# Decode attention with a gated FFN: splitting TensorE's value pass around the first tile's scores, and moving the last semaphore clear

## The chip, the cores and the metric

The kernel runs on one core of a Trainium2 chip. The metric is the device time of one execution in microseconds (us), as the median of several runs. A separate execution was taken with the hardware profiler; its times are used wherever a single instruction or a stretch of the run is spoken of. One core has TensorE (PE, matrix products into PSUM), VectorE (DVE), ScalarE (ACT), GpSimd (POOL) and SyncE (SP, which here only issues DMAs). All engines run on their own and meet at semaphores.

## The reference

One token `x` (512 values) goes through two branches that are mixed by a scalar gate.

```python
q = (x @ wq) as 32 heads of 128
scores = einsum("bhqd,bhkd->bhqk", q, k_cache) * 128 ** -0.5     # 32 heads x 65536 keys
p = softmax(scores); o = einsum("bhqk,bhkd->bhqd", p, v_cache)   # 65536 values of 128 per head
a = o.reshape(1, 1, 4096) @ wo
b = (silu(x @ w_gate) * (x @ w_up)) @ w_down
out = g * a + (1 - g) * b,   g = sigmoid(sum(x * gate_w))
```

Everything is bfloat16. The two caches are 537 MB each (32 x 65536 x 128 x 2 bytes), and every byte of them is read once.

## The kernel before: how the work is tiled and staged

A **tile** is 16384 keys of one head (128 partitions x 128 keys x 128 values of a key), and four tiles make a head. Two tiles make a **pair**, 8.39 MB, and a head is two pairs. There are 128 tiles and 64 pairs for K and as many for V. On chip there are two K buffers of a pair each (`K_bufs`) and one V buffer of a pair (`V_buf`, in two halves of 4.19 MB).

**Scores of a tile** (VectorE, then TensorE, then VectorE). `product` (L264) multiplies the tile by the head's query, in place. `add_halves` (L275) adds the upper half of the 128 products of each key to the lower one: 128 to 64, to 32, and the last time to 16 columns, which go into a small tile `T_sb`. `scores` (L446) lets TensorE add those 16 columns in groups of four, by four matmuls with a unit matrix, into `S_ps`, and `fold` (L286) adds the last four columns on VectorE and writes the scores to `S_sb`. `T_sb` is a single buffer: the last addition of a tile waits for the scores of the tile before (`wait(dve, pe_S, n)`).

**Softmax and values** run one head behind the scores. VectorE takes the head's maximum (L292), TensorE turns it (L460), ScalarE makes the exponentials of two tiles at a time (`P_sb`, L365), and TensorE multiplies them by V: `values` (L467) is 32 matmuls for each half of V, so 64 for a pair.

**TensorE runs a loop** (`tensor_step`) of 61 turns, one for each pair from the third to the last but one. Within a turn its order is fixed, and `take(credit)` makes the whole engine wait for another engine's credit: first `c_S[0]` (tile 0's `T_sb`), then `c_q`, `c_P` (the exponentials), `c_V` twice (a half of V has landed; GpSimd passes this on, `tell_of_v`), `c_S[1]` (tile 1's `T_sb`), `c_o` and `c_m`.

**SP issues all large DMAs in a fixed order** on one queue. In the turn for pair m, `sync_step` issues the V load of pair m - 1, then the K load of pair m + 2. K's load (L174) waits until both tiles' scores of pair m are made, since it takes the place of that pair. V's load differs by parity. For a pair with an **even** number one DMA of 8.39 MB (L174) waits until *both* halves of the V pair before have been used. For an **odd** one two DMAs of 4.19 MB (L178) go out as each half comes free. In this order the queue sees, over one head: V (whole pair), K, V (half), V (half), K.

```python
    def load_v(i):
        for n in (2 * i, 2 * i + 1):
            wait(sync, pe_V, n - 1 if i % 2 else 2 * i)
            if i % 2:
                load_tile(V_half[n % 2], A_v_cache, n, (vA_in, vB_in)[n % 2])
        if i % 2 == 0:
            load_pair(V_buf, A_v_cache, i, vA_in)
```

The turns thus come in two kinds, which the text calls by what TensorE reads in them. In the **pair turn** V comes in one DMA of 8.39 MB, and behind it the two half loads are issued; in the **halves turn** V comes in two DMAs, and behind it the whole pair is issued.

**Start and end.** The prologue makes q, the gate, the FFN and the first four tiles' scores. `tensor_end` does the last pair with its own finer loads, projects with `wo`, and SP stores 1 KB of output (L230). Then GpSimd waits for three engines and for the output's landing, and clears all semaphores (L692).

Of the kernel before, what the change touches and what calls it, by code (L numbers as in the profile page):

```python
# [11 lines left out]
NB = 128  # L12
# [29 lines left out]
def kernel(  # L42
# [14 lines left out]
    nc = tc.nc  # L57
# [21 lines left out]
    def sb(name, shape, dtype=f32):  # L79
        return consts.tile(shape, dtype, name=name)  # L80
# [11 lines left out]
    P_sb = sb("P_sb", [P, PAIR], bf16)  # L92
# [33 lines left out]
    def halves(buf):  # L126
        return [buf[:, i * NB * Dh : (i + 1) * NB * Dh].rearrange("p (j d) -> p j d", d=Dh) for i in range(2)]

    K_half, V_half = [halves(b) for b in K_bufs], halves(V_buf)
# [3 lines left out]
    def v_view(n):  # L133
        return {N - 4: K_half[0][1], N - 3: V_half[0], N - 2: V_half[1], N - 1: K_half[1][1]}[n]

    sync, act, dve, pool, pe = nc.sync, nc.scalar, nc.vector, nc.gpsimd, nc.tensor
    first_sem = nc.alloc_semaphore("first")
    done = Events(nc, "done")
    po, pe_x, pe_S, pe_V, pe_q, pe_m, pe_t, pe_o = (
        Events(nc, n) for n in ("po", "pe_x", "pe_S", "pe_V", "pe_q", "pe_m", "pe_t", "pe_o")  # L140
    )
    ac, ac_q, dv, dv_top, dv_max, dv_rg = (
        Events(nc, n) for n in ("ac", "ac_q", "dv", "dv_top", "dv_max", "dv_rg")
    )
    x_in, gw_in, wq_in, kb_in, wg_in, wu_in, wd_in, vA_in, vB_in, out_in = (
        Events(nc, n, 16)
        for n in ("x_in", "gw_in", "wq_in", "kb_in", "wg_in", "wu_in", "wd_in", "vA_in", "vB_in", "out_in")
    )
    k_in = [Events(nc, f"k{i}_in", 16) for i in range(2)]
    v4_in = Events(nc, "v4_in", 16)  # L150
# [5 lines left out]
    c_q, c_P, c_V, c_o, c_m = (nc.alloc_semaphore(n) for n in ("c_q", "c_P", "c_V", "c_o", "c_m"))  # L156
# [4 lines left out]
    def wait(engine, events, value):  # L161
        key = id(engine), id(events)
        if seen.get(key, 0) < value:
            engine.wait_ge(events.sem, value)
            seen[key] = value
# [40 lines left out]
    def sync_step(m):  # L206
        load_v(m - 1)
        if m + 2 < M:
            wait(sync, pe_S, 2 * m + 2)
            load_k(m + 2)  # L210
# [16 lines left out]
    def sync_out():  # L227
        wait(sync, dv, dv.n)
        wait(sync, ac, ac.n)
        out_in(sync.dma_start(out=out[0], in_=out_sb))  # L230


    def unit_matrix():
# [19 lines left out]
    def product(n):  # L253
        K = K_half[n // 2 % 2][n % 2]
        q = q_sb[n // G % 2]
        q_rep = bass.AP(tensor=q.tensor, offset=q[:, :].offset, ap=[list(q[:, :].ap[0]), [0, NB], [1, Dh]])
        m = n // 2

        if m in (0, M - 1) and n % 2:
            wait(dve, kb_in, 16 if m == 0 else 32)  # L260
        else:
            wait(dve, k_in[m % 2], 16 * (m // 2 + 1))
        wait(dve, ac_q, n // G + 1)
        return dv(dve.tensor_tensor(out=K, in0=K, in1=q_rep, op=ALU.mult))  # L264

    def add_halves(n, width, last, out=None):
        K = K_half[n // 2 % 2][n % 2]
        half, mark = Dh // 2, last
        while half >= width:
            wait(dve, dv, mark)  # L270
            to = K[:, :, 0:half]
            if half == width and out is not None:
                wait(dve, pe_S, n)
                to = out
            ins = dve.tensor_tensor(out=to, in0=K[:, :, 0:half], in1=K[:, :, half : 2 * half], op=ALU.add)  # L275
            if half == width and out is not None:
                ins.then_inc(c_S[n % 2], 1)
            else:
                mark = dv(ins)
            half //= 2  # L280
        marks["K", n] = mark

    def fold(n):
        h, g = divmod(n, G)
        wait(dve, pe_S, n + 1)
        return dv(dve.tensor_reduce(  # L286
            out=S_sb[h % 2][:, g * NB : (g + 1) * NB], in_=S_ps[n % 2], axis=AXIS.X, op=ALU.add
        ))

    def row_max(h, folded):  # L290
        wait(dve, dv, folded)
        dv_max(dve.tensor_reduce(out=m_sb[:, 0:1], in_=S_sb[h % 2], axis=AXIS.X, op=ALU.max))  # L292

    def top_of(h):
        wait(dve, pe_m, 2 * h + 1)
        dv_top(dve.tensor_reduce(out=top[:, 0:1], in_=mT, axis=AXIS.X, op=ALU.max))  # L296

    def weight(h, t):
        wait(dve, pe_t, t)
        if h < H - 1:  # L300
            wait(dve, dv, dv(dve.tensor_reduce(out=tsum[:, 0:1], in_=tot, axis=AXIS.X, op=ALU.add)))
            total = tsum[:, 0:1]
        else:
            total = tot[:, 0:1]
        wait(dve, dv, dv(dve.reciprocal(recip[:, 0:1], total)))
        dv_rg(dve.tensor_tensor(out=rg[:, h : h + 1], in0=recip[:, 0:1], in1=gval, op=ALU.mult))

    def vector_step(m):
        h, b = divmod(m, MH)
        width, to = (WIDTH, T_sb) if m < M - 1 else (LAST, None)  # L310
        last = product(2 * m)
        if b == 0:
            top_of(h - 1)
        else:
            fold(2 * m - 1)
        add_halves(2 * m, width, last, to)
        last = product(2 * m + 1)
        fold(2 * m)
        if b == 1:
            weight(h - 1, m - 1)  # L320
        add_halves(2 * m + 1, width, last, to)
        if b == 1:
            row_max(h, fold(2 * m + 1))

    def vector_end():
        top_of(H - 1)
        weight(H - 1, M - 1)
        wait(dve, pe_x, 5)
        dv(dve.tensor_copy(out=out_sb[:, :HD], in_=a_ps[0]))  # L329
# [71 lines left out]
    def scalar_step(m):  # L401
        h, b = divmod(m, MH)
        if b == 0:
            head_bias(h - 1)
        wait(act, pe_V, 2 * (m - 2))
        exponentials(h - 1, b, P_sb, PAIR).then_inc(c_P, 1)
        if m == M - 1:
            return
        if b == 1:
            query(h + 1, True)  # L410
        else:
            act.sem_inc(c_q, 1)
        wait(act, pe_V, 2 * (m - 2) + 2)
        o_copy(h - 1).then_inc(c_o, 1)
        wait(act, pe_o, m - 1)
        if b == 0:
            marks["half_o"] = ac(copy(half_o[:, 0:1], oh))
            act.sem_inc(c_m, 1)
        else:
            ac(head_out(h - 1, add_half_o()))  # L420
            head_diag(h, True)
# [18 lines left out]
    def take(credit):  # L440
        pe.wait_ge(credit, 1)
        pe.sem_inc(credit, -1)  # L442

    def scores(n, src, width):
        for c in range(0, width, QUAD):
            ins = pe.matmul(  # L446
                S_ps[n % 2], lhsT=ident_b, rhs=src[:, :, c : c + QUAD],
                start=(c == 0), stop=(c == width - QUAD),
            )
        pe_S(ins)  # L450
# [5 lines left out]
    def query_spread():  # L456
        pe_q(pe.matmul(qb, lhsT=ones_b, rhs=q_diag, start=True, stop=True))  # L457

    def max_turn():
        pe_m(pe.matmul(mT, lhsT=ones_f, rhs=diag, start=True, stop=True))  # L460

    def total(n=2):
        pe_t(pe.matmul(tot[:, :n], lhsT=ones_f, rhs=rs[:, :n], start=True, stop=True))  # L463

    def values(probs, view, start, stop, opens, closes):
        for j in range(start, stop, 4):
            ins = pe.matmul(  # L467
                O_ps, lhsT=probs[:, j : j + 4], rhs=view[:, j : j + 4, :],
                start=(opens and j == start), stop=(closes and j == stop - 4),
            )  # L470
        return ins

    def head_turn(opens=True):
        for c in range(4):
            ins = pe.matmul(  # L475
                oh, lhsT=O_sb[:, c * Dh : (c + 1) * Dh], rhs=ident_f[0:4, c : c + 1],
                start=(opens and c == 0), stop=(c == 3),
            )
        pe_o(ins)
# [124 lines left out]


    def tensor_step():
        take(c_S[0])
        scores(0, T_sb, WIDTH)
        take(c_q)
        query_spread()  # L610
        take(c_P)
        total()
        for i in range(2):
            take(c_V)
            pe_V(values(P_sb[:, i * NB : (i + 1) * NB], V_half[i], 0, NB, i == 0, i == 1))
        take(c_S[1])
        scores(1, T_sb, WIDTH)
        take(c_o)
        head_turn()
        take(c_m)  # L620
        max_turn()
# [50 lines left out]
    with tc.tile_critical():  # L672
        prologue()
        for m in range(2, M):
            vector_step(m)
            scalar_step(m)
            if m < M - 1:
                sync_step(m)
            tell_of_v(m - 2)
        sync_end()  # L680
        scalar_end()
        vector_end()
        sync_out()
        with pe.Fori(0, M - 3):
            tensor_step()
        tensor_end()
        for engine in (pe, act, dve):
            engine.sem_inc(done.sem, 1)

        pool.wait_ge(done.sem, 3)  # L690
        pool.wait_ge(out_in.sem, 16)
        pool.sem_clear(range(first_sem.num, last_sem.num + 1))  # L692


# [28 lines left out]
```

## Time and profile before

| | |
|---|---|
| median of 3 runs | 2542.01 us (2541.46 to 2542.71) |
| the profiled execution's own time | 2539.18 us |
| its span, first to last instruction | 2537.4 us |
| VectorE busy | 2217.8 us, 87% |
| TensorE busy (matmuls) | 1334.6 us, 53% |
| DMA: queue q1 (SP) | 1087.65 MB, 99.6% of the 16 engines' span |

The profiled execution ran 2.8 us under the median, and 1.8 us of its time lie outside its span. A row of a timeline gives start, duration, engine, line, operation, output and inputs, and, in square brackets, how long the engine had been idle and who released it. "<-PEq" is TensorE's own sequencer, which is where a `take` shows. In the table of windows, PEclk is the granted TensorE clock as a share of the full one, and the last column is what the DMA engines moved. SPq rows are DMA issues; they stand at the moment at which SP issued, not when the data landed.

### The profile page before, as it was taken

Reading aid. Unit: us, or ns where it says so; the run is one execution under the profiler, and the core shown is the slowest. Engines: PE = TensorE matmul, PEld = TensorE weight load, DVE = VectorE, ACT = ScalarE, POOL = GpSimd, SP = SyncE. Lnnn points to the kernel's source line nnn. Section 1 sums busy time; section 2 is a strip of 40 time slices with the busy share of each in tenths; the row PEclk is TensorE's granted clock in tenths of the full one; section 3 lists DMA queues with packets and bytes.
Section 4 is the critical chain, followed back from the end, with each engine's and each line's share of the span. In section 5 each row is a group of like instructions: output and inputs, shape, how many; then the busy total and the mean of one; then the engine's idle time right before and its main releaser. Section 6 shows DMA issues by size and latency. Waiting matters only on the chain. (4 is left out here: it accounts for less than half of the span.)

```text
span 2537.4 us, 14083 instructions
## 1 busy us (share of the span) xinstructions
PE 1334.6 (53%) x5813; PEld 557.8 (22%) x5813; DVE 2217.8 (87%) x802; ACT 187.8 (7%) x503; POOL 0.7 (0%) x6
## 2 busy tenths in 40 slices
PE   2644645546446455464564554654645646446459
PEld 1212212212112122121221221221212212212124
DVE  5898888988988988889898898898898988988992
ACT  0000000000000000000000000000000000000000
POOL 0000000000000000000000000000000000000000
PEclk8767767677677677676776777767767767677679
DMA  9999999999999999999999999999999999999998
GB/s 413 433 442 431 432 430 422 429 426 430 438 428 429 438 425 434 427 422 426 430 431 430 434 438 433 431 430 429 432 440 420 439 421 426 435 430 433 433 423 378
DMA packets 26853, 1087.85 MB, mean 429 GB/s; under 512 B 3153, under 2 KB 3666, under 8 KB 4946
## 3 DMA queue, kind: packets, MB, share of 16 engines
q1 hardware_dynamic: 26546, 1087.65, 99.6%
q8 instruction: 5, 0.08, 0.0%
q14 instruction: 14, 0.11, 0.0%
q10 hardware_dynamic: 288, 0.00, 0.0%
HBM read 1087.64 MB, written 0.00 MB: 429 GB/s over the span
## 5 line engine op out<-in xcount | busy, mean ns | idle before, releaser
L264 DVE TENSOR_TENSOR K_buf<-K_buf,q_sb 128x16384 bf16<-128x16384 bf16 x128 | 1112.1, 8688 | 214.0 <-DMA K_buf<-in_A_k_cache_dram 214.0
L467 PE MATMUL O_ps<-V_buf,P_sb 128*4 128x512 bf16 x3968 | 957.0, 406 | 24.6 <-PEq L442 24.6
L275 DVE TENSOR_TENSOR K_buf<-K_buf 128x8192 bf16<-128x8192 bf16 x252 | 849.5, 3371 | 4.3
L446 PE MATMUL S_ps<-T_sb,ident_b 128*128 128x512 bf16 x488 | 180.0, 505 | 1033.9 <-PEq L442 1033.6
L467 PEld LDWEIGHTS O_ps<-V_buf,P_sb 128*4 128x4 bf16 x3968 | 349.9, 89 | 603.0 <-issue 159.5
L446 PEld LDWEIGHTS S_ps<-T_sb,ident_b 128*128 128x128 bf16 x488 | 44.9, 110 | 1123.7 <-issue 1107.5
L333 ACT ACTIVATE O_sb<-O_ps 4x512 f32<-4x512 f32 x63 | 63.5, 1008 | 1290.3 <-PE O_ps L467 1290.3
L275 DVE TENSOR_TENSOR T_sb<-K_buf 128x2048 bf16<-128x2048 bf16 x122 | 149.4, 1224 | 4.2
L286 DVE TENSOR_REDUCE S_sb<-S_ps 128x128 f32<-128x512 f32 x128 | 87.8, 686 | 48.0 <-PE S_ps L446 48.0
L460 PE MATMUL qm_ps<-diag,ones_f 128*128 128x128 f32 x126 | 34.0, 357 | 69.8 <-PEq L442 67.7
L475 PE MATMUL oh_ps<-ident_f,O_sb 4*128 4x1 f32 x504 | 64.6, 245 | 9.0 <-PEq L442 8.2
L475 PEld LDWEIGHTS oh_ps<-ident_f,O_sb 4*128 4x128 f32 x504 | 60.7, 186 | 38.6 <-issue 38.2
L333 ACT ACTIVATE q_sb<-qm_ps 128x128 bf16<-128x128 f32 x32 | 8.9, 278 | 585.7 <-PE qm_ps L457 585.7
L446 PE MATMUL S_ps<-K_buf,ident_b 128*128 128x512 bf16 x80 | 28.6, 529 | 42.8 <-DVE K_buf L275 35.1
L460 PEld LDWEIGHTS qm_ps<-diag,ones_f 128*128 128x128 f32 x126 | 21.8, 217 | 74.1 <-issue 71.1
L463 PEld LDWEIGHTS tot_ps<-rs,ones_f 128*128 128x128 f32 x126 | 34.1, 330 | 18.0 <-issue 17.9
L333 ACT ACTIVATE oT<-whole_o,rg 32x1 bf16<-32x1 f32 (+1 forms) x115 | 33.9, 295 | 2.0
L463 PE MATMUL tot_ps<-rs,ones_f 128*128 128x2 f32 (+1 forms) x126 | 33.1, 333 | 0.0
L365 ACT ACTIVATE P_sb<-S_sb,bias 128x256 bf16<-128x256 f32 x62 | 31.5, 509 | 1.2 <-issue 0.2
L333 ACT ACTIVATE bias<-top 128x1 f32<-128x1 f32 x32 | 6.5, 203 | 266.8 <-DVE top L296 266.8
L329 DVE CAST out_sb<-a_ps 1x256 bf16<-1x256 f32 x1 | 0.4, 413 | 27.2 <-PE a_ps L484 27.2
L292 DVE TENSOR_REDUCE m<-S_sb 128x1 f32<-128x512 f32 x32 | 22.0, 686 | 1.1
(60 smaller groups left out, 197.9 us busy)
## 6 DMA issues: line engine op xcount, KB each, us to landing
V_buf<-in_A_v_cache_dram SPq DMA_DIRECT2D x62, 4096.0 KB, 21.3
K_buf<-in_A_k_cache_dram SPq DMA_DIRECT2D x4, 4096.0 KB, 32.8
V_buf<-in_A_v_cache_dram SPq DMA_DIRECT2D x4, 2048.0 KB, 19.5
V_buf<-in_A_wq_dram SPq DMA_DIRECT2D x1, 4096.0 KB, 12.4
K_buf<-in_A_v_cache_dram SPq DMA_DIRECT2D x1, 4096.0 KB, 36.1
K_buf<-in_A_v_cache_dram SPq DMA_DIRECT2D x3, 1024.0 KB, 25.1
K_buf<-in_A_wo_dram SPq DMA_DIRECT2D x1, 2048.0 KB, 26.8
V_buf<-in_B_w_gate_dram SPq DMA_DIRECT2D x1, 1792.0 KB, 54.7
```

The source lines that it names most:

```text
L264: return dv(dve.tensor_tensor(out=K, in0=K, in1=q_rep, op=ALU.mult))
L275: ins = dve.tensor_tensor(out=to, in0=K[:, :, 0:half], in1=K[:, :, half : 2 * half], op=ALU.add)
L286: return dv(dve.tensor_reduce(out=S_sb[h % 2][:, g * NB : (g + 1) * NB], in_=S_ps[n % 2], axis=AXIS.X, op=ALU.add))
L292: dv_max(dve.tensor_reduce(out=m_sb[:, 0:1], in_=S_sb[h % 2], axis=AXIS.X, op=ALU.max))
L329: dv(dve.tensor_copy(out=out_sb[:, :HD], in_=a_ps[0]))
L333: return act.activation(out=out, in_=in_, func=ACT.Copy, scale=scale)
L365: return act.activation(out=out, in_=S_sb[h % 2][:, b * PAIR : b * PAIR + count], func=ACT.Exp, bias=bias[:, 0:1], scale=scale, accum_out= ...
L446: ins = pe.matmul(S_ps[n % 2], lhsT=ident_b, rhs=src[:, :, c : c + QUAD], start=(c == 0), stop=(c == width - QUAD),)
L460: pe_m(pe.matmul(mT, lhsT=ones_f, rhs=diag, start=True, stop=True))
L463: pe_t(pe.matmul(tot[:, :n], lhsT=ones_f, rhs=rs[:, :n], start=True, stop=True))
L467: ins = pe.matmul(O_ps, lhsT=probs[:, j : j + 4], rhs=view[:, j : j + 4, :], start=(opens and j == start), stop=(closes and j == stop - 4),)
L475: ins = pe.matmul(oh, lhsT=O_sb[:, c * Dh : (c + 1) * Dh], rhs=ident_f[0:4, c : c + 1], start=(opens and c == 0), stop=(c == 3),)
```

## The change: what it does

Three edits. **TensorE's loop:** the total and the first half of V now come ahead of tile 0's scores; the second half stays behind them. **VectorE:** the fold of tile 0 moves from ahead of tile 1's additions to just before the last of them. **The end:** SP tells GpSimd that the output has been issued, GpSimd clears the semaphores at that, and SP itself waits for the landing and takes the output's semaphore, now outside the cleared range, back to zero.

```diff
-    def add_halves(n, width, last, out=None):
+    def add_halves(n, width, last, out=None, ahead=None):
...
             to = K[:, :, 0:half]
+            if half == width and ahead is not None:
+                fold(ahead)
             if half == width and out is not None:
                 wait(dve, pe_S, n)
...
         last = product(2 * m + 1)
-        fold(2 * m)
         if b == 1:
             weight(h - 1, m - 1)
-        add_halves(2 * m + 1, width, last, to)
+        add_halves(2 * m + 1, width, last, to, 2 * m)
...
     def tensor_step():
+        take(c_P)
+        total()
+        take(c_V)
+        pe_V(values(P_sb, V_half[0], 0, NB, True, False))
         take(c_S[0])
         scores(0, T_sb, WIDTH)
         take(c_q)
         query_spread()
-        take(c_P)
-        total()
-        for i in range(2):
-            take(c_V)
-            pe_V(values(P_sb[:, i * NB : (i + 1) * NB], V_half[i], 0, NB, i == 0, i == 1))
+        take(c_V)
+        pe_V(values(P_sb[:, NB:], V_half[1], 0, NB, False, True))
         take(c_S[1])
         scores(1, T_sb, WIDTH)
...
         out_in(sync.dma_start(out=out[0], in_=out_sb))
+        sync.sem_inc(done.sem, 1)
...
-        pool.wait_ge(done.sem, 3)
-        pool.wait_ge(out_in.sem, 16)
+        pool.wait_ge(done.sem, 4)
         pool.sem_clear(range(first_sem.num, last_sem.num + 1))
+        sync.wait_ge(out_in.sem, 16)
+        sync.sem_inc(out_in.sem, -16)
```

`out_in` is now allocated ahead of `first_sem`, so that the clear does not touch it. No instruction on data is added or taken away on any engine; on the DMA queue the transfers, their sizes and their order stay as they were.

More of the change, by code (lines that the diff above doesn't have):

```diff
@@ L136 @@
     sync, act, dve, pool, pe = nc.sync, nc.scalar, nc.vector, nc.gpsimd, nc.tensor
+    out_in = Events(nc, "out_in", 16)
     first_sem = nc.alloc_semaphore("first")
@@ L144 @@
     )
-    x_in, gw_in, wq_in, kb_in, wg_in, wu_in, wd_in, vA_in, vB_in, out_in = (
+    x_in, gw_in, wq_in, kb_in, wg_in, wu_in, wd_in, vA_in, vB_in = (
         Events(nc, n, 16)
-        for n in ("x_in", "gw_in", "wq_in", "kb_in", "wg_in", "wu_in", "wd_in", "vA_in", "vB_in", "out_in")
+        for n in ("x_in", "gw_in", "wq_in", "kb_in", "wg_in", "wu_in", "wd_in", "vA_in", "vB_in")
     )
```

## The prediction

> **What bounds the kernel now.** I read the page first: busy shares, then DMA queues, then the costliest groups.
>
> ```profile
> PE 1334.6 (53%) x5813; PEld 557.8 (22%) x5813; DVE 2217.8 (87%) x802; ACT 187.8 (7%) x503; POOL 0.7 (0%) x6
> ...
> DMA packets 26853, 1087.85 MB, mean 429 GB/s; under 512 B 3153, under 2 KB 3666, under 8 KB 4946
> ...
> q1 hardware_dynamic: 26546, 1087.65, 99.6%
> ...
> L264 DVE TENSOR_TENSOR K_buf<-K_buf,q_sb 128x16384 bf16<-128x16384 bf16 x128 | 1112.1, 8688 | 214.0 <-DMA K_buf<-in_A_k_cache_dram 214.0
> ```
>
> No engine is full, VectorE waits 214.0 us for K, and the DMA queue looks full at 99.6%. Is it full at its best rate? The table of windows, in stretches of 400 us, says no:
>
> ```profile
> 900.00:1300.00 400.00, 206.63 (x867) 85.49 (x865) 352.66 (x126) 32.30 (x85) 0.00 (x0) 0.72 1.00 427
> 1400.00:1800.00 400.00, 212.49 (x898) 88.06 (x896) 358.67 (x134) 32.74 (x87) 0.00 (x0) 0.73 1.00 433
> ```
>
> The DMA share is 1.00 both times, yet the rate (last column) differs by 1.4%: in the slower stretch packets took longer. I looked for the place in one head of it. The issues, from SP's timeline:
>
> ```profile
> 1017.57 0.33 SPq L174 DMA_DIRECT2D V_buf<-in_A_v_cache_dram  x1
> 1018.59 0.33 SPq L174 DMA_DIRECT2D K_buf<-in_A_k_cache_dram  x1
> 1051.05 7.23 SPq L178 DMA_DIRECT2D V_buf<-in_A_v_cache_dram  x2
> 1058.98 0.33 SPq L174 DMA_DIRECT2D K_buf<-in_A_k_cache_dram  x1
> 1096.15 0.33 SPq L174 DMA_DIRECT2D V_buf<-in_A_v_cache_dram  x1
> ```
>
> VectorE's timeline, where a product released by DMA marks the landing of a K pair:
>
> ```profile
> 1021.19 8.69 DVE L264 TENSOR_TENSOR K_buf<-K_buf,q_sb 128x16384 bf16<-128x16384 bf16 x1 [1.18 <-DMA K_buf<-in_A_k_cache_dram]
> ...
> 1061.17 8.69 DVE L264 TENSOR_TENSOR K_buf<-K_buf,q_sb 128x16384 bf16<-128x16384 bf16 x1 [6.06 <-DMA K_buf<-in_A_k_cache_dram]
> ...
> 1077.16 1.22 DVE L275 TENSOR_TENSOR T_sb<-K_buf 128x2048 bf16<-128x2048 bf16 x1
> ...
> 1099.82 8.69 DVE L264 TENSOR_TENSOR K_buf<-K_buf,q_sb 128x16384 bf16<-128x16384 bf16 x1 [1.18 <-DMA K_buf<-in_A_k_cache_dram]
> ```
>
> And TensorE's:
>
> ```profile
> 1041.93 16.00 PE L467 MATMUL O_ps<-V_buf,P_sb 128*4 128x512 bf16 x64 [1.49 <-PEq L442]
> ...
> 1078.53 1.86 PE L446 MATMUL S_ps<-T_sb,ident_b 128*128 128x512 bf16 x4 [17.67 <-PEq L442]
> ...
> 1080.75 15.37 PE L467 MATMUL O_ps<-V_buf,P_sb 128*4 128x512 bf16 x64
> 1096.11 1.08 PE L446 MATMUL S_ps<-T_sb,ident_b 128*128 128x512 bf16 x4
> ```
>
> The reader is to see a loop. When SP issues the whole V pair at 1017.57, all that is left in the queue is the end of the K pair that VectorE takes 3.6 us later. V and the next K follow; K lands at 1061.17, tile 0's `T_sb` is ready at 1078.4, TensorE does its scores, then all 64 value matmuls, and only then, at 1096.15, is the next V pair issued, 78.58 us after the first, and again 3.7 us ahead of K's landing. In the trace's packet records the first of the 16 engines runs dry 0.4 to 1 us after an issue as late as this, and the next packets take up to 4.2 us instead of the median 2.418 (64 KB). Within -4 to +10 us of the 30 whole-pair issues, idle time and excess over the median duration come to 17.8 us; around the half-pair issues, made some 10 us ahead of K's landing, there is next to none.
>
> Three heads show a fed queue. There V was issued 4.7 and 4.3 us ahead (1407.80 and 1485.76), and K landed at
>
> ```profile
> 1412.54 8.69 DVE L264 TENSOR_TENSOR K_buf<-K_buf,q_sb 128x16384 bf16<-128x16384 bf16 x1 [1.25 <-DMA K_buf<-in_A_k_cache_dram]
> ...
> 1644.70 8.69 DVE L264 TENSOR_TENSOR K_buf<-K_buf,q_sb 128x16384 bf16<-128x16384 bf16 x1 [0.63 <-DMA K_buf<-in_A_k_cache_dram]
> ```
>
> three heads in 232.16 us, **77.39 us a head**, which is 33.55 MB at 433.6 GB/s. From 162.84 to 2424.43, 29 heads took 2261.6 us, **77.99 a head**.
>
> **The change, part by part.** *TensorE's order, halves turn* (times from the K landing at 1061.17). Tile 0's `T_sb` is ready at +17.2. The first V half needs no `T_sb`: it lands one half transfer (4.19 MB at 433.6 GB/s, 9.7 us) into the turn, and the exponentials are there by then (ScalarE made them around 1060). Of the 64 matmuls of a pair the last 32 run at some 0.215 us, 6.9 together, so the first 32 take 16.0 - 6.9 = 9.1 us, slow clock at the start included. They end at about +20; scores 0 and the query end at +21.5; the second half has landed at +19.4 and ends at about +28. The whole V pair is therefore issued at +28 instead of +35.0, 10.6 us ahead of K's landing instead of 3.7. That is the lead at which the half pairs lose nothing. I take the loss down to that of the three best-fed issues (0.04 to 0.10 us each, say 0.05).
>
> *Pair turn* (from 1021.19). V starts at +20.7 as before; its first half ends at +29.8, where the half load goes out as before (+29.9). Scores 0 now come behind it and end at +31 instead of +18.8: this is the wait that the change adds. Queued behind it are the fold of tile 0 and, through the single `T_sb`, tile 1's last addition. In the old place VectorE would have stood from +25.3 to +31, 5.7 us; in the new place it arrives at 1053.89 - 1021.19 = +32.7, 1.7 us after the scores. So nothing waits, and were that cover gone, each us of delay would first eat the 6.06 us for which VectorE waits for K at 1061.17. The second half then ends at +38.2 (the second half load goes out 1.4 us later) and tile 1's scores at +39.3 (K's issue, 1.5 later). The K pair in transfer lands at +40 and the first half load behind it covers the queue to +49.7. Cost nothing.
>
> *VectorE* has the same instructions, in all 72 us a head against 77.4. *Tile 1's scores, halves turn:* TensorE now idles from +28 to +35 before them. After such gaps the row at 1078.53 shows 1.86 us for four matmuls, without a gap 1.08; K's issue may come 0.8 us later, covered by the 19.4 us of V ahead of it.
>
> *The end.* The output is issued at 2534.93; 1.2 us later GpSimd sees it landed, and the clear (0.31 us) and a drain stand between that and the last barrier. With the clear inside the landing's shadow I take 0.3 us off; bounds 0 and 0.7.
>
> *Sum.* By landings, 29 x (77.99 - 77.39) = 17.3 us; by packet records, 17.8 - 30 x 0.05 = 16.3. I take 16.8, plus 0.3: 17.1. The profiled execution goes from 2539.2 to 2522.1, its span from 2537.4 to 2520.3; the median, 2.8 us above the profiled one, from 2542.0 to **2525 us**. For comparison, the Trainium skill ("DMA: Bandwidth & Descriptors", specifications) puts the fabric's ceiling at 435 GB/s, 77.1 us a head; by that the estimate would be 8 us lower, but 77.39 is what fed heads here took.
>
> **Rivals.** *Part of it:* the queue gets dry elsewhere, say at the second half load or at K's later issue, or first packets stay slow. A third to two thirds of 17: 2531 to 2537, about 2534. Against it: leads of 9 us and more at all other issues.
>
> *No effect:* the slow packets have another cause (reading memory, say), and only happen to fall behind the whole-pair issue. Then only the end's 0.3 us show: 2541.7. Against it: the loss follows the lead, 0.04 to 0.30 us where the first engine still had 2.5 us of work, 0.5 to 1.3 where it had under 1.
>
> *Slower:* in the pair turn TensorE becomes the last. Its second half now ends at +38; the half load needs issue by about +47 (2.5 us before +49.7). If the split bursts ran at the half clock throughout, 64 matmuls at 0.427 with 1.9 us of scores between them end at 20.7 + 27.3 + 1.9 + 0.3 = +50.2, and the queue stands dry for about 3 us a head: 30 x 3 = 90 us, 2632. It decides from 9 us of delay. Against it: the granted clock reaches 1.00 within 4 to 6 us of each burst's start, and the scores only fill the burst.
>
> *Cold scores:* a smaller mechanism on the same side. If K's later issue in the halves turn did set the landing, 30 heads would lose 30 x 0.78 = 23 us, more than the gain: 2542 - 17 + 23 = 2548. Against it: the V pair ahead of K in the queue. The Trainium skill ("TensorE: Matmul & The Clock Gate", section "Why this matters for your kernels") advises against TensorE gaps of over about 3 us between bursts, since the clock then falls to half; the trace agrees (granted clock 0.50 from 1024 to 1044).
>
> **How the numbers follow.** Forecast 0.76, its own range 2522.5 to 2530 (an unremoved loss of 0.2 us an issue is 6 us less, the floor by packet medians 1.5 more). Part of it 0.08, no effect 0.08, slower by TensorE 0.05, cold scores 0.03. The range of 2522.5 to 2534 leaves out about half of "part of it" and all of the last three. A measurement here can tell 0.2% (5.1 us) from no change: faster than that 0.83, same 0.09, slower 0.08.
>
> **What would show it.** In the new profile the whole-pair issue should stand 9 to 11 us ahead of the landing of K instead of 3.6; K landings should be 77.4 us a head throughout; windows of 400 us should all show 433; VectorE's fold of tile 0 should show no wait for scores. The forecast is wrong if landings stay near 78.0 with the early issue (slow packets of another cause), if the fold waits for scores in every pair turn, or if the second half load comes within 2 us of the queue's end.

## The result, and the profile after

The changed kernel takes **2524.55 us** (median of 4 runs, 2523.8 to 2525.28) beside 2541.74 us for the kernel before (4 runs, 2536.8 to 2542.71). The ratio is 0.9936, with a 95% interval of 0.9919 to 0.9953: 0.64% faster, 17.2 us by the medians. The profiled execution took 2523.84 us with a span of 2522.0 us, 15.4 us less than that of before. The kernel before varies more from run to run than the changed one: over all series taken for this study it lay between 2536.1 and 2547.9 us, the changed one between 2523.8 and 2525.6. So the gain in a single pair of executions can be read as anything from 11 to 24 us; the medians say 17, the two profiles 15.4.

From the page of the changed kernel:

```profile
PE 1388.8 (55%) x5813; PEld 574.9 (23%) x5813; DVE 2220.4 (88%) x802; ACT 187.2 (7%) x503; POOL 0.7 (0%) x6
...
DMA packets 26854, 1087.85 MB, mean 431 GB/s; under 512 B 3154, under 2 KB 3667, under 8 KB 4947
...
q1 hardware_dynamic: 26546, 1087.65, 99.7%
...
L266 DVE TENSOR_TENSOR K_buf<-K_buf,q_sb 128x16384 bf16<-128x16384 bf16 x128 | 1112.0, 8688 | 173.5 <-DMA K_buf<-in_A_k_cache_dram 173.5
```

The same bytes moved at a higher mean rate, and VectorE waits 40 us less for K. TensorE shows 54 us *more* busy time for the same matmuls (418 ns for a value matmul in the mean, 406 before), and that cost nothing. In the table of windows the slow stretches are gone; the six windows of 400 us from 100 to 2500 us show 432 to 435 GB/s, where before they showed 427 to 432. Two of them:

```profile
900.00:1300.00 400.00, 215.29 (x863) 87.89 (x864) 361.79 (x129) 30.22 (x81) 0.00 (x0) 0.71 1.00 434
1300.00:1700.00 400.00, 225.74 (x910) 91.39 (x907) 361.76 (x132) 30.54 (x82) 0.00 (x0) 0.73 1.00 435
```

One head in the three timelines, SP first:

```profile
1002.83 0.33 SPq L175 DMA_DIRECT2D V_buf<-in_A_v_cache_dram  x1
1012.40 0.33 SPq L175 DMA_DIRECT2D K_buf<-in_A_k_cache_dram  x1
1042.81 8.40 SPq L179 DMA_DIRECT2D V_buf<-in_A_v_cache_dram  x2
1051.91 0.33 SPq L175 DMA_DIRECT2D K_buf<-in_A_k_cache_dram  x1
1080.73 0.33 SPq L175 DMA_DIRECT2D V_buf<-in_A_v_cache_dram  x1
1089.70 0.33 SPq L175 DMA_DIRECT2D K_buf<-in_A_k_cache_dram  x1
```

VectorE's, with the fold of tile 0 (L290) in its new place in the pair turn:

```profile
1014.25 8.69 DVE L266 TENSOR_TENSOR K_buf<-K_buf,q_sb 128x16384 bf16<-128x16384 bf16 x1 [0.43 <-DMA K_buf<-in_A_k_cache_dram]
...
1046.48 0.69 DVE L290 TENSOR_REDUCE S_sb<-S_ps 128x128 f32<-128x512 f32 x1
...
1052.87 8.69 DVE L266 TENSOR_TENSOR K_buf<-K_buf,q_sb 128x16384 bf16<-128x16384 bf16 x1 [4.57 <-DMA K_buf<-in_A_k_cache_dram]
...
1089.71 0.69 DVE L290 TENSOR_REDUCE S_sb<-S_ps 128x128 f32<-128x512 f32 x1 [2.05 <-PE S_ps L449]
...
1091.56 8.69 DVE L266 TENSOR_TENSOR K_buf<-K_buf,q_sb 128x16384 bf16<-128x16384 bf16 x1 [0.44 <-DMA K_buf<-in_A_k_cache_dram]
```

And TensorE's, in both kinds of turn:

```profile
1033.72 9.06 PE L470 MATMUL O_ps<-V_buf,P_sb 128*4 128x512 bf16 x32 [9.01 <-PEq L445]
1042.71 1.09 PE L449 MATMUL S_ps<-T_sb,ident_b 128*128 128x512 bf16 x4
...
1062.71 9.91 PE L470 MATMUL O_ps<-V_buf,P_sb 128*4 128x512 bf16 x32 [8.37 <-PEq L445]
1072.56 1.09 PE L449 MATMUL S_ps<-T_sb,ident_b 128*128 128x512 bf16 x4
...
1073.63 7.07 PE L470 MATMUL O_ps<-V_buf,P_sb 128*4 128x512 bf16 x32
1087.81 1.87 PE L449 MATMUL S_ps<-T_sb,ident_b 128*128 128x512 bf16 x4 [7.11 <-PEq L445]
```

The reader is to see that the whole V pair now goes out at 1080.73, 10.8 us ahead of the landing at 1091.56, and that two landings of the same kind are 1091.56 - 1014.25 = 77.31 us apart instead of 78.6. This head has nearly the shortest lead of the run: over the 30 whole-pair issues behind the first one it is 10.8 to 12.7 us, 11.6 in the mean, where before it was 3.1 to 5.2, 3.9 in the mean. In the packet records, idle time and slow packets around the 30 whole-pair issues come to 0.24 us, where they were 17.8.

The chain that ended last has changed too. Before, it ran through the last loads of the output projection. Now, from the landing of the last but one K pair on, it holds VectorE and TensorE, and three short steps of ScalarE (0.4 to 0.6 us each, not shown):

```profile
2369.60 39.71 DMA K_buf<-in_A_k_cache_dram
...
2409.34 8.69 DVE K_buf L266
...
2443.39 8.60 DVE K_buf L266
...
2475.63 1.92 PE S_ps L449 x8
...
2493.65 20.30 PE O_ps L470 x94
...
2515.66 3.60 PE a_ps L487 x32
```

That gives a way to take every run apart in three pieces: the last but one K pair's product starts (here 2409.3), from there to the output's issue (110.4), and from there to the last instruction (2.28). Before, they were 2424.4, 110.5 and 2.43.

### The profile page after: what moved, and what is told of

Read it like the earlier page. It is cut to its first block, busy times and chain, and to the rows that moved or that the text cites. A ratio compares the mean times of both kernels' runs of the same rounds, so it can differ in the third digit from the quotient of the medians.

```text
span 2522.0 us, 14146 instructions
## 1 busy us (share of the span) xinstructions
PE 1388.8 (55%) x5813; PEld 574.9 (23%) x5813; DVE 2220.4 (88%) x802; ACT 187.2 (7%) x503; POOL 0.7 (0%) x6
## 5 line engine op out<-in xcount | busy, mean ns | idle before, releaser
L470 PE MATMUL O_ps<-V_buf,P_sb 128*4 128x512 bf16 x3968 | 1006.7, 418 | 519.6 <-PEq L445 519.3
L266 DVE TENSOR_TENSOR K_buf<-K_buf,q_sb 128x16384 bf16<-128x16384 bf16 x128 | 1112.0, 8688 | 173.5 <-DMA K_buf<-in_A_k_cache_dram 173.5
L449 PE MATMUL S_ps<-T_sb,ident_b 128*128 128x512 bf16 x488 | 156.3, 449 | 240.0 <-PEq L445 240.0
L290 DVE TENSOR_REDUCE S_sb<-S_ps 128x128 f32<-128x512 f32 x128 | 88.3, 690 | 71.8 <-PE S_ps L449 69.7
L478 PEld LDWEIGHTS oh_ps<-ident_f,O_sb 4*128 4x128 f32 x504 | 85.9, 253 | 46.6 <-issue 46.1
L478 PE MATMUL oh_ps<-ident_f,O_sb 4*128 4x1 f32 x504 | 90.5, 296 | 6.1 <-PEq L445 5.7
L466 PEld LDWEIGHTS tot_ps<-rs,ones_f 128*128 128x128 f32 x126 | 25.7, 254 | 244.5 <-issue 244.4
L399 ACT ACTIVATE whole_o<-oh_ps,half_o 128x1 f32<-128x1 f32 x31 | 8.1, 261 | 317.9 <-PE oh_ps L478 317.9
L449 PEld LDWEIGHTS S_ps<-K_buf,ident_b 128*128 128x128 bf16 x80 | 9.4, 123 | 60.0 <-DVE K_buf L279 45.0
```

The source lines that it names most:

```text
L290: return dv(dve.tensor_reduce(out=S_sb[h % 2][:, g * NB : (g + 1) * NB], in_=S_ps[n % 2], axis=AXIS.X, op=ALU.add))
L399: wait(act, ac, ac(act.activation(out=whole_o[:, 0:1], in_=oh, func=ACT.Identity, bias=half_o[:, 0:1], scale=1.0)))
L449: ins = pe.matmul(S_ps[n % 2], lhsT=ident_b, rhs=src[:, :, c : c + QUAD], start=(c == 0), stop=(c == width - QUAD),)
L470: ins = pe.matmul(O_ps, lhsT=probs[:, j : j + 4], rhs=view[:, j : j + 4, :], start=(opens and j == start), stop=(closes and j == stop - 4),)
L478: ins = pe.matmul(oh, lhsT=O_sb[:, c * Dh : (c + 1) * Dh], rhs=ident_f[0:4, c : c + 1], start=(opens and c == 0), stop=(c == 3),)
```

## The experiments

The theory: what counts is how far ahead of K's landing the queue gets the whole V pair, the **lead**; nothing else in the change matters but for VectorE's fold, which has to follow TensorE's order. The rivals: TensorE's order helps by itself, the end carries part of the gain, or the slow packets had another cause. The times come in three series, each from one chip with the kernel before beside it: `order_only`, `end_only`, `halves_old_order` and `pair_last`; `pair_mid`, `fold_old_place`, `halves_new_order` and `no_late_wo`; `after_again`, `tail_weight` and `tail_lean`.

**The parts alone.** `order_only` is the changed kernel with the old end (`out_in` is cleared with the others again):

```diff
-        sync.sem_inc(done.sem, 1)
...
-        pool.wait_ge(done.sem, 4)
+        pool.wait_ge(done.sem, 3)
+        pool.wait_ge(out_in.sem, 16)
         pool.sem_clear(range(first_sem.num, last_sem.num + 1))
-        sync.wait_ge(out_in.sem, 16)
-        sync.sem_inc(out_in.sem, -16)
```

> TensorE's new order and VectorE's later fold, with the old end. Theory (the gain is the whole pair's earlier issue, the end is worth some 0.15 us): 2524 to 2526, within 0.5 us of the changed kernel; loss around the 30 whole-pair issues under 0.5 us. Rival (the end carries a good part): 2528 or more.

Measured: 2524.11 us (5 runs, 2523.95 to 2525.4), ratio 0.9931 (0.9917 to 0.9944). `end_only` is the kernel before with that edit the other way round:

> The old order everywhere, the new end alone. Theory: no measurable change, 2541 to 2542 (0.1 to 0.3 us off the path from the output's issue to the last instruction: 2.43 us before, 2.28 us in the changed kernel). Rival (the end carries a good part): 2538 or less.

Measured: 2541.69 us (11 runs, 2538.81 to 2547.12) beside 2540.72 for the kernel before, ratio 1.0006 (0.9996 to 1.0015). The time from the output's issue to the last instruction is 2.28 us with the new end and 2.43 with the old, in either order. So the end is worth 0.15 us and the order all the rest.

**The lead without TensorE's order.** `halves_old_order` is the kernel before, with V loaded by halves in both kinds of turn:

```diff
         for n in (2 * i, 2 * i + 1):
-            wait(sync, pe_V, n - 1 if i % 2 else 2 * i)
-            if i % 2:
-                load_tile(V_half[n % 2], A_v_cache, n, (vA_in, vB_in)[n % 2])
-        if i % 2 == 0:
-            load_pair(V_buf, A_v_cache, i, vA_in)
+            wait(sync, pe_V, n - 1)
+            load_tile(V_half[n % 2], A_v_cache, n, (vA_in, vB_in)[n % 2])
```

(GpSimd's credits follow: one for each half.)

> TensorE's and VectorE's old order and the old end, but V always comes in two half loads, each issued as its half comes free. Theory (what counts is how far ahead of K's landing the queue is refilled): the first half goes out some 10 us ahead of K's landing in the halves turn too, the loss goes, 2524 to 2527. Rival (what counts is TensorE's order, or that the scores no longer stand ahead of the values): 2539 to 2542.

Measured: 2525.57 us (5 runs, 2524.23 to 2525.75), ratio 0.9933 (0.9919 to 0.9947). SP's timeline shows why, beside VectorE's row for the landing of K:

```profile
1081.71 7.23 SPq L178 DMA_DIRECT2D V_buf<-in_A_v_cache_dram  x2
1089.64 0.33 SPq L174 DMA_DIRECT2D K_buf<-in_A_k_cache_dram  x1
```

```profile
1091.89 8.69 DVE L261 TENSOR_TENSOR K_buf<-K_buf,q_sb 128x16384 bf16<-128x16384 bf16 x1 [0.84 <-DMA K_buf<-in_A_k_cache_dram]
```

The first half goes out 10.2 us ahead, with TensorE and VectorE in the old order, and the gain is there. TensorE's order is one way to get the lead and not a cause of its own. The run by itself leaves one rival: in the packet records all of V now comes in packets of 32 KB, where the whole pairs had 64. The next runs keep the whole pairs as they are.

**Less lead in the changed kernel.** `pair_last` and `pair_mid` hold the whole V pair back on SP:

```diff
         if i % 2 == 0:
+            wait(sync, pe_S, 2 * i + 4)                # pair_last: tile 1's scores
+            wait(sync, dv, marks["K", 2 * i + 3])      # pair_mid, in its place: tile 1 added to 32 columns
             load_pair(V_buf, A_v_cache, i, vA_in)
```

> The changed kernel, but the whole V pair is issued only when tile 1's scores are made, just ahead of K's load: 1.9 us ahead of K's landing instead of 10.8. Theory (lead): the queue runs dry at each of the 30 issues, for more than the 0.3 to 1.3 us that a lead of 3.6 us cost before: 1.5 to 2.2 us each, 2565 to 2590. Rival (slow packets of another cause, to which the new order put an end): 2524 to 2526.

> The changed kernel, but the whole V pair is issued only when VectorE has added tile 1 to 32 columns, some 5.7 us ahead of K's landing (changed kernel 10.8, before 3.6, whole pair last 1.9). Theory (a lead of some 4 us or more loses nothing, since the slow packets come only when an engine has run dry): 2524 to 2527. Rival (the longer the lead, the better, in proportion): about 2535.

Measured: `pair_last` 2558.42 us (4 runs, 2550.28 to 2560.87), ratio 1.0054 (1.0036 to 1.0072); `pair_mid` 2525.45 us (4 runs, 2525.16 to 2526.06), ratio 0.9934 (0.9918 to 0.9949). In `pair_last` the issue stands this far from the landing:

```profile
1106.69 0.33 SPq L175 DMA_DIRECT2D V_buf<-in_A_v_cache_dram  x1
1107.06 0.43 SPq L175 DMA_DIRECT2D K_buf<-in_A_k_cache_dram  x1
```

```profile
1108.51 8.69 DVE L267 TENSOR_TENSOR K_buf<-K_buf,q_sb 128x16384 bf16<-128x16384 bf16 x1 [0.45 <-DMA K_buf<-in_A_k_cache_dram]
```

1.8 us, and 1.3 to 2.7 over the run. K's own load goes out about where it did (1.5 us ahead of the landing, 1.9 in the changed kernel). The losses of `pair_last` around the 30 issues come to 37.7 us, 1.26 each, and a head takes 78.67 us (mean from the seventh to the 63rd K pair); I had expected 1.5 to 2.2 each, so the direction holds and the price was set too high. This is the strongest run of the study: TensorE's order and VectorE's are those of the changed kernel, and the kernel is slower than before. With 5.7 us of lead (`pair_mid`, below) a head takes 77.50 us, in the changed kernel 77.48.

```profile
1085.95 0.33 SPq L175 DMA_DIRECT2D V_buf<-in_A_v_cache_dram  x1
```

```profile
1091.63 8.69 DVE L267 TENSOR_TENSOR K_buf<-K_buf,q_sb 128x16384 bf16<-128x16384 bf16 x1 [0.44 <-DMA K_buf<-in_A_k_cache_dram]
```

| lead of the whole V pair, mean of 30 issues, us | kernel | us a head | loss around 30 issues, us |
|---|---|---|---|
| 2.0 | pair_last | 78.67 | 37.7 |
| 3.9 | before | 78.01 | 17.8 |
| 5.7 | pair_mid | 77.50 | 3.7 |
| 11.6 | changed | 77.48 | 0.2 |

Within one kernel, the loss at an issue follows less the lead itself than what the first of the 16 engines then has left to do. In `pair_last` it is 2.4 to 2.7 us at the four issues that came 0.9 us or more after that engine had run dry, and 0.4 to 0.8 at the three where it had over a microsecond of work. About a third of the loss of before is idle time (5.6 us), the rest slow packets (12.0). Why packets behind a late issue are slow, no run shows.

`halves_new_order` goes the other way: the changed kernel with V always by halves, the same edit as above.

> The changed kernel with V always in two half loads. Theory (the queue already loses only 0.2 us over all 30 issues): no change against the changed kernel, 2523.5 to 2526. Rival (the lead is still worth something): 2522 or less.

Measured: 2525.21 us (5 runs, 2524.92 to 2526.43), ratio 0.9933 (0.9919 to 0.9946). No more is to be had from the lead.

**VectorE's fold.** `fold_old_place` takes back that part alone:

```diff
         last = product(2 * m + 1)
+        fold(2 * m)
...
-        add_halves(2 * m + 1, width, last, to, 2 * m)
+        add_halves(2 * m + 1, width, last, to)
```

> TensorE's new order, but VectorE folds tile 0 in the old place, right behind tile 1's product. In the pair turn the fold then waits for the scores behind V's first half: 3.1 us a head by the changed kernel's rows (product ends at 1039.7, scores at 1043.7), 4 us at most. Theory (VectorE has 4.6 us of slack there, and DMA is the bound): 2524 to 2527. Rival (VectorE is near enough to its limit that the wait shows): 10 us or more slower than the changed kernel.

Measured: 2528.91 us (5 runs, 2528.78 to 2529.5), ratio 0.9948 (0.9934 to 0.9962): slower than the changed kernel by 4.4 us by the medians and 5.1 by the profiles, between what theory and rival expected. VectorE's timeline in mid-run and in the last pair turn:

```profile
1014.34 8.69 DVE L266 TENSOR_TENSOR K_buf<-K_buf,q_sb 128x16384 bf16<-128x16384 bf16 x1 [0.37 <-DMA K_buf<-in_A_k_cache_dram]
...
1044.26 0.69 DVE L290 TENSOR_REDUCE S_sb<-S_ps 128x128 f32<-128x512 f32 x1 [4.50 <-PE S_ps L450]
...
1052.94 8.69 DVE L266 TENSOR_TENSOR K_buf<-K_buf,q_sb 128x16384 bf16<-128x16384 bf16 x1
...
2408.57 8.69 DVE L266 TENSOR_TENSOR K_buf<-K_buf,q_sb 128x16384 bf16<-128x16384 bf16 x1 [0.30 <-DMA K_buf<-in_A_k_cache_dram]
...
2439.91 0.69 DVE L290 TENSOR_REDUCE S_sb<-S_ps 128x128 f32<-128x512 f32 x1 [5.93 <-PE S_ps L450]
...
2448.44 8.69 DVE L266 TENSOR_TENSOR K_buf<-K_buf,q_sb 128x16384 bf16<-128x16384 bf16 x1
```

In mid-run the fold waits 4.5 us (3.1 to 4 had been expected), and the next product starts where it did without that wait (1052.94 against 1052.87): the slack for K has been spent, no more. Over the whole run VectorE waits 47.8 us for K, where the changed kernel has 173.5, so little slack is left. The landings keep their pace (77.45 us a head), and the last but one K pair is even 0.8 us earlier than in the changed kernel. In the last pair turn there is no K to wait for, since the last pair has long been loaded; the 5.9 us go straight into the end. From the last but one product to the output's issue it is 116.3 us instead of 110.4. So moving the fold is worth nothing in 30 of its 31 pair turns and 4.4 (by the medians) to 5.9 us (by this interval) in the last one.

**What sets the end now.** `no_late_wo` leaves out the last four loads of the output projection, and TensorE's waits for them, so that heads 16 to 31 are projected with stale numbers:

```diff
-        for a, b in zip(LATE_CUTS[:-1], LATE_CUTS[1:]):
-            load_wo(a, b)
...
         for a, b in zip(LATE_CUTS[:-1], LATE_CUTS[1:]):
-            wait(pe, wo_in[a], 16)
```

> The changed kernel without the last four loads of the output projection (2.1 MB, 4.8 us of the queue) and without the waits for them: heads 16 to 31 are projected with what lies in the buffer. Theory (since the change the end hangs on VectorE and TensorE, the queue is done some 7 us before the last matmul): at most 0.5 us less than the changed kernel, 2523.5 to 2525. Rival (the queue still sets the end): 4 to 5 us less, 2519 to 2520.5.

Measured: 2523.74 us (5 runs, 2523.49 to 2523.91), ratio 0.9927 (0.9914 to 0.9941). The last packet of the projection's loads ends at 2516.1 us in the changed kernel; here the queue is done by 2511.1, and the output's issue stays where it was (110.42 us after the last but one product, 110.41 in the changed kernel). The queue no longer sets the end.

**Shortening that end.** `after_again` is the changed kernel on the same chip as the next two:

> The changed kernel once more, beside the two that follow. 2523.5 to 2525.5.

Measured: 2523.86 us (5 runs, 2523.8 to 2525.56), ratio 0.9937 (0.9923 to 0.995). `tail_weight` moves three small VectorE operations in the last pair:

```diff
-        if b == 1:
+        if b == 1 and m < M - 1:
             weight(h - 1, m - 1)
...
             row_max(h, fold(2 * m + 1))
+            if m == M - 1:
+                weight(h - 1, m - 1)
```

> The changed kernel, but in the last pair VectorE makes the weight of the head before (three small operations, 0.46 us from start to start) after the last maximum instead of ahead of tile 1's additions, where it is behind TensorE's turn of the maximum. Theory (since the change VectorE's chain of the last two pairs and TensorE behind it set the end): 0.4 to 0.5 us less than the changed kernel. Rival (the end hangs on something else): no change, within 0.2 us.

Measured: 2523.66 us (5 runs, 2523.2 to 2524.95), ratio 0.9934 (0.9921 to 0.9948). `tail_lean` also lets TensorE project four heads ahead of the last turn:

```diff
+        wait(pe, wo_in[EARLY], 16)
+        project(EARLY, EARLY + 4)
         wait(pe, ac, marks["O_last"])
         head_turn(opens=False)
+        project(EARLY + 4, LATE_CUTS[1])
-        for a, b in zip(LATE_CUTS[:-1], LATE_CUTS[1:]):
+        for a, b in zip(LATE_CUTS[1:-1], LATE_CUTS[2:]):
```

> As tail_weight, and TensorE projects four heads (0.9 us) while ScalarE copies the last head's values, where TensorE stood for 0.6 us before the last turn. Theory: another 0.4 to 0.6 us less, 0.8 to 1.1 in all against the changed kernel, about 2523.5. Rival (the loads of the output projection, which end near 2516, stand in the way): no more than tail_weight.

Measured: 2523.21 us (5 runs, 2523.12 to 2524.47), ratio 0.9932 (0.9918 to 0.9945). By the time from the last but one product to the output's issue, 110.42 us became 110.08 and then 109.81: 0.34 and 0.27 us, each less than expected but in its place. The medians go the same way, yet their ranges overlap, so `tail_lean` is the fastest kernel of the study by a little that the times alone don't prove.

## Why the prediction was right, point by point

The forecast was 2525, the result 2524.55; the mechanism was the one forecast.

*The loop through the whole V pair's issue.* Right. The lead rose from 3.6 to 10.8 us in the heads shown, as forecast (10.6), and from 3.9 to 11.6 in the mean; its losses went from 17.8 to 0.24 us (1.5 had been left for them). That the lead is the cause is shown by `halves_old_order` and `pair_last`, not only by the timing of the change.

*TensorE's bursts.* The first half took 9.06 us in the pair turn and 9.91 in the halves turn (9.1 forecast), the second 7.07 (6.9).

*The wait that the change adds.* Right that nothing waits: the fold at 1046.48 stands without idle time, 2.7 us after the scores were done. The step that said what it would cost if that cover were gone was incomplete. It gave VectorE's slack for K as the next cover, which holds for every pair turn but the last. There `fold_old_place` paid 5.9 us. VectorE's 72 us a head were a little high: the rows of before give 71.4 (39.98 and 38.65 us less the 6.06 and 1.18 for which it waits for K).

*Cold scores.* As forecast, tile 1's scores in the halves turn run at the low clock (granted clock 0.50 from 1087.8 to 1089.7, 7.1 us after the values ended; 1.87 us for four, from 1.08) and VectorE's fold waits 2.05 us instead of 1.26. It is hidden behind K's landing, which still comes 0.4 us later. The Trainium skill ("TensorE: Matmul & The Clock Gate", section "Why this matters for your kernels") is right that the gap lowers the clock. The time did not follow, since TensorE isn't the bound here.

*The sum.* Two terms were mis-sized. The 29 heads were to gain 16.8 us. They took 2246.0 us instead of 2261.6, 15.6 less, and 77.45 us a head where the forecast had 77.39: three well-fed heads (one of them with a lead of only 3.7 us) were too few to read a floor from to 0.06 us. The other way to the same term, by packet records, averages the loss over 16 engines, while a landing waits for the last of them. From the first to the last of these landings the mean of the engines gained 18.3 us (2261.2 to 2242.9), the last engine 14.9 (2261.7 to 2246.8). A head's bytes in median packets, the bound that the forecast named, come to 77.44 us. That this meets the landings is chance: the engine done first took 77.32 us a head (2242.2 / 29), the last one 77.47, and what held it up is told in the last section. The end brought 0.15 us, not 0.3: SP's own wait for the landing and the drains behind it still stand there, and only the clear has moved into its shadow. Besides, the product at the start of these heads came 0.5 us later than before (163.35 against 162.84) with its K already there: VectorE was the last here, behind the cold scores, for which the sum had no term. So the last but one K pair came 15.1 us earlier, and the span, forecast at 2520.3, came to 2522.0. That the median came out at 2525 all the same is partly luck: the profiled execution of before lay 2.8 us under its median, that of the changed kernel only 0.7.

*The rivals.* "Part of it" and "no effect" are out by the packet records. "TensorE becomes the last" did not come near: the second half load goes out 8.1 us after the first in every head, 10.7 us or more before the first one's transfer ends (K's landing and 9.7 us).

## What to carry to other kernels

A queue that shows 99.6% busy can still lose time (here 17.8 of 2537 us): look at the rate in long windows and at the time between an issue and the landing ahead of it, and find the issue that comes last. When all loads go through one queue in a fixed order, only the issue with the shortest lead needs to go out earlier. Here it made no difference whether another order on the engine that frees the buffer or loads by halves brought that about, and 5.7 us of lead were nearly as good as 11.6. A wait that is free in the steady state because a transfer covers it is paid in the last turn, where there is nothing left to wait for.

## What the runs showed of the hardware that was not expected

Sixteen engines that never run dry drift apart. In the changed kernel the first of them was done with a K pair 1.7 us before the last one at 151 us, and 6.2 us before at 2398 us, in the packet records; before, it was 1.1 to 3.1 us throughout. The records show what holds the last engine up. Between 200 and 2400 us there are 13 loads of instructions (queue q14, 8 KB and 0.31 us each), and 13 data packets that took over 0.1 us longer than the median (0.24 to 0.54 us); each of these starts within 0.4 us behind the start of one of the loads. The distance between the first and the last engine grew by some 0.84 us (0.31 + 0.53) at each of the loads of 863, 1243, 1592, 1948 and 2290 us. As far as its packets can be told from the others', the engine that ends last in `order_only` had met seven such loads and the first one none. Late issues seem to hide this, since the other engines run dry and wait while the last one catches up; what the time would be without these loads was not tried. The first engine's lead at the whole-pair issue so fell from 9.9 to 4.4 us over the run, while SP issued 10.8 to 12.7 us ahead of the landing throughout. In `pair_mid`, with 5.7 us of lead, it fell to 1.3 to 2.5 us, and from 1396 us on losses came back at some issues (up to 0.86 us at one).

The changed kernel's runs fall on two levels, about 2523.8 and 2525.3. In profiled executions of the kernels here, the same two levels stand between the last but one product and the output's issue (110.4 and 111.8 us), and they come with the clock of the last eight score matmuls: 1.90 us for the eight in the changed kernel, 3.40 in `halves_old_order`, 2.61 in `pair_mid`. Just before these eight, TensorE had idled for 1.33 us in the changed kernel, 2.43 and 2.06 us in the other two. Why TensorE's clock falls there in some executions and not in others was not tried.
